# RWKV5 attention and a SoLU feed-forward on one core: the first nine chunks and the first pair written as one flat list of calls, with another order of the first loads

## The chip, the core and the metric

The kernel runs on one core of a Trainium2 chip. A core has a matrix engine (TensorE, PE in the profile, its weight loads PEld), a vector engine (DVE), a scalar engine (ACT), GpSimd (POOL) and a sync engine (SP), which in this kernel only issues DMAs. Each engine runs its own instructions in order and waits on semaphores for the others. The metric is the time of one launch in microseconds on the device.

## The reference

Attention first, then a feed-forward block on its output; B=4 batches, H=8 heads, S=768 steps, D=48 per head, all in float32 but the weights, which the kernel reads as pairs of 32-bit words:

```python
for t in range(S):                       # w: decay per head and dim, u: bonus
    kt, vt, rt = k[:, :, t], v[:, :, t], r[:, :, t]
    cur = einsum('bhd,bhe->bhde', u[None] * kt, vt)
    y[:, :, t] = einsum('bhd,bhde->bhe', rt, state + cur)
    state = w[None, :, :, None] * state + einsum('bhd,bhe->bhde', kt, vt)
x = y.transpose(0, 2, 1, 3).reshape(B * S, H * D)      # 3072 x 384
h = x @ w_in                                           # 3072 x 1024
sm = exp(h - max(h)) / sum(exp(h - max(h)))
solu = h * sm
ln = (solu - mean(solu)) / sqrt(var(solu) + 1e-6) * g_ln
out = ln @ w_out                                       # 3072 x 384
```

## The kernel before

**Tiles.** The 3072 rows are 24 chunks of 128: six stretches of a sequence by four batches, batches inside. Chunk i is worked on by a chain of small functions, each of which puts a few instructions on the engines. The lines are those of the profile.

- `load(i, "kr")` and `load(i, "v")` (L473, L478) put the DMAs of chunk i's k, r and v on SP's queue, into one of five `kpad`, one of five `rpad` and one of six `vt` tiles. k and r are 192 KB each, v is 192 KB, or two halves of 96 KB from chunk 4 on.
- `decay_k(i)` (GpSimd, L702) multiplies k by the table `kdec` into `kp`; `weigh(i)` (GpSimd, L715 and L716) makes `rku` = k·u·r; `sum_own(i)` (DVE, L720) sums it to `own`, the diagonal of the scores. `decay_r(i)` (GpSimd, L709) is used from chunk 9 on.
- `turn_r(i)` and `turn_k(i)` (PE, L759 and L767) transpose r and `kp`; DVE multiplies r by the table `fore` (L760), ACT copies k (L769). From chunk 9 on (`FIRST`), `halve_k`, `halve_r` and `join_rk` do this with a DMA transpose instead.
- `diagonal(i)` writes `own` onto a diagonal in a tile `big`: on ACT, 8 copies at L730, for the first four chunks (`WHOLE`), on GpSimd, 2 selects at L735, for the others.
- `whole_scores(i)` (PE, L782) or `scores(i)` (PE, L800) make the scores in PSUM, in the tile `at`, and `take_scores(i)` (DVE, `copy_predicated`, L808 or L813) copies those above the diagonal into `big`. There is one `at`, with two places used from chunk 8 on: the scores of a later chunk wait until it is read.
- `whole_y(i)` or `merged_y(i)` (PE, L839, L856) make y, ACT copies it (`take_y`, L867). `whole_outer(i)` or `outer(i)` (PE, L892, L883) make the state's increment `kv`; `middle(i)` (DVE, L904) and `update(i)` (DVE, L917, L919, and GpSimd, L922, with the tile `wide`) move the state on.
- `ffn_in(j)` (PE, L932, six matmuls of 128x512) makes h, and ACT its exponential `e` (L937). `unit_a` (DVE, L942, L944) and `unit_b` (ACT, L951, L952) make `solu` and its sums, `deviation` (GpSimd, L960) the deviations.
- `halve_ln(j)` (ACT, L986) splits `solu` in 16-bit halves and sends them through a DMA transpose (L975, on SP's queue), `join_ln(j)` (DVE, L980) puts them together, and `ffn_out(j)` (PE, L1025) multiplies by `w_out` and stores the result.
- The weights come in 14 pieces, 0 to 5 of `w_in` (512 KB each), 6 to 13 of `w_out` (384 KB): `load_weights(p)` (SP, L519), then `convert_a(p)` (ACT, L530, the low words), `convert_b(p)` (DVE, L543 and L545, the high words), `convert_c(p)` (GpSimd, L553, the sum) and, for `w_out`, `convert_d(p)` (the scale of the layer norm, on DVE L564 or ACT L561).
- Before the chunks, DVE builds the tables `back` and `fore` from the decays by repeated squares (L630 to L641), `turn_table` (PE, ACT, L651, L652) turns them to `kdec` and `rdec`, and `spin(n)` (L605) puts n small matmuls with no use of their result on PE.

**Order.** The program says `tc.manual_schedule()`: no planner moves anything. Every engine takes its instructions in the order in which the calls stand in the text, and SP's queue takes the DMAs in that order. The text has these parts: the first loads, the tables, a hand-written list for chunks 0 to 2, a loop over i = 2 to 6 that brings chunks 3 to 7 in and in which the `w_out` pieces are converted, a hand-written list for the first pair (chunks 7 and 8, with chunk 5's and 6's h and the first two results), and a loop over the remaining pairs. The loop over i has, for example,

```python
load(i + 5, "kr")
load(i + 4, "v")
if i > LA:
    ffn_in(j)
```

and so on, so that chunk i+5's loads are issued while chunk i+2's k and r are turned and chunk i-2's h is made. The loads ahead of the first chunks are

```python
load(0, "kr"); load_weights(0); load(1, "kr"); load(0, "v"); load_weights(1); load(2, "kr")
load_weights(2); load(1, "v"); load_weights(3); load_weights(4); load_weights(5)
load(3, "kr"); load(2, "v"); load(4, "kr")
```

(the text has one call to a line). Each is one or two DMAs on SP's queue, and `wq`, the decays, is loaded on the same queue ahead of them.

Of the kernel before, what the change touches and what calls it, by code (L numbers as in the profile page):

```python
# [9 lines left out]
F32 = mybir.dt.float32  # L10
U32 = mybir.dt.uint32
ACT = mybir.ActivationFunctionType
ALU = mybir.AluOpType
# [386 lines left out]
def direct_path(  # L400
# [87 lines left out]
    w_out_sb = const.tile([128, KF, dm], F32, name="w_out_sb")  # L488
    decays = const.tile([128, HP], F32, name="decays")

    nc.vector.memset(wq, 1.0)
    nc.sync.dma_start(out=wq[:, :, 0:D], in_=w.rearrange("(a q) d -> a q d", q=2))
    u_row = u_bc[0:1].rearrange("p h d -> p (h d)")
    nc.scalar.dma_start(out=u_row, in_=u.rearrange("h d -> (h d)").unsqueeze(0))
    for i in range(NLD):
# [20 lines left out]
    def load_weights(j, tag="raw", bufs=6):  # L516
        dst, src, _ = pieces[j]
        raws[j] = wpool.tile([128, dst.shape[1], 2], U32, tag=tag, name="raw", bufs=bufs)
        nc.sync.dma_start(out=raws[j].rearrange("p n o -> p (n o)"), in_=src)  # L519
# [58 lines left out]


    load(0, "kr")  # L580
    load_weights(0)
    load(1, "kr")
    load(0, "v")
    load_weights(1)
    load(2, "kr")
    load_weights(2)
    load(1, "v")
    load_weights(3)
    load_weights(4)
    load_weights(5)  # L590
    load(3, "kr")
    load(2, "v")
    load(4, "kr")
    nc.sync.dma_start(out=g_sb, in_=moe_g_ln.rearrange("(c p) -> p c", p=128))

# [30 lines left out]
    for vt in vts:  # L626
        nc.scalar.activation(out=vt[:, 1].rearrange("p h x -> p (h x)"),
                             in_=ident[:, 0:1].to_broadcast([128, H * P]), func=ACT.Copy, scale=0.0)
    spin(3)
    nc.vector.tensor_scalar(out=pw[:, 0, 0], in0=wd_ps, scalar1=LOW, scalar2=HIGH,  # L630
                            op0=ALU.max, op1=ALU.min)
    nc.vector.tensor_copy(out=decays, in_=wd_ps)
    for j in range(8):
        if j < 7:
            nc.vector.tensor_mul(pw[:, 0, j + 1], pw[:, 0, j], pw[:, 0, j])
# [117 lines left out]
            nc.scalar.copy(out=X["G"][0:D, 1, :, q, :], in_=X["rT"][rows, :, U:T])  # L753

    def turn_r(i):
        rT = factors(i)["rT"]
        ps = psM.tile([128, HP, T], F32, tag="m", name="tr_ps")
        for a in range(HP):
            nc.tensor.transpose(ps[:, a, :], pair(rpads[i % NLD], a), ident)  # L759
        nc.vector.tensor_mul(rT, ps, fore)  # L760

    def turn_k(i):
        X = live[i]
        ps = psM.tile([128, HP, T], F32, tag="m", name="tk_ps")

        for a in range(HP):
            nc.tensor.transpose(ps[:, a, :], pair(X["kp"] if i > 0 else kpads[0], a), ident)  # L767
        if i > 0:
            nc.scalar.copy(out=X["kT"], in_=ps)  # L769
        else:  # L770
            nc.vector.tensor_mul(X["kT"], ps, back)
# [132 lines left out]
            nc.vector.tensor_add(mid(i)[:, :, q], X["kv"][0][q * P : q * P + D],  # L904
                                 carried(i)[:, :, q])

    def update(i):
        b, c = units[i]
        if c == C - 1:
            return  # L910
        X = live[i]
        for q in range(2):
            rows = slice(q * P, q * P + D)
            wT = pw[rows, 0, 7].unsqueeze(2).to_broadcast([D, HP, D])
            new = carried(i + B)[:, :, q]
            if i < WHOLE:
                nc.vector.tensor_mul(new, X["kv"][rows], wT)  # L917
            else:
                nc.vector.tensor_add(new, X["kv"][1][rows], mid(i)[:, :, q])  # L919
        if i >= WHOLE:  # L920
            S = vts[(i + B) % NV][P : P + D, 0, :, 0:D]
            nc.gpsimd.tensor_mul(S, S, wide[P : P + D].unsqueeze(2).to_broadcast([D, H, D]))  # L922


    def ffn_in(i, halves=(0, 1)):
        X = live[i]
        if 0 in halves:
            X["h"] = psH.tile([128, dff], F32, tag="h", name="h_ps")
        h_ps = X["h"]
        for n in halves:  # L930
            for j in range(KD):
                nc.tensor.matmul(h_ps[:, ts(n, NX)], X["xT"][:, j, :], w_in_sb[:, j, ts(n, NX)],  # L932
                                 start=(j == 0), stop=(j == KD - 1))
        if 1 not in halves:
            return
        e = X["e"] = fpool.tile([128, dff], F32, name="e", bufs=1)
        nc.scalar.activation(out=e, in_=h_ps, func=ACT.Exp, accum_out=sums[:, i : i + 1])  # L937

# [41 lines left out]
        nc.vector.tensor_copy(out=words.bitcast(U16).rearrange("p n (t o) -> p o n t", o=2),  # L980
                              in_=turned)

    def halve_ln(i):
        X = live[i]
        both = halves()
        nc.scalar.copy(out=both.rearrange("p (o n) -> p o n", o=2), in_=split(X["solu"]))  # L986
        X["turned"] = turn(both)

    def join_ln(i):
        X = live[i]  # L990
# [49 lines left out]
        for i in chunks:  # L1040
            middle(i)

    ahead = 6

    def take_up(p, more=1):
        nonlocal ahead
        convert_a(p)
        for _ in range(more):
            if ahead < len(pieces):
                load_weights(ahead)  # L1050
                ahead += 1

    turn_r(0)
    turn_k(0)
    turn_table(back, kdec, psM.tile([128, HP, 128], F32, tag="m", name="kd_ps"))
    weigh(0, nc.gpsimd)
    decay_k(0)
    sum_own(0)
    diagonal(0)
    take_up(0)  # L1060
    spin(2)
    whole_scores(0)
    convert_b(0)
    decay_k(1)
    weigh(1, nc.gpsimd)
    turn_r(1)
    spin(4)
    turn_k(1)
    take_scores(0)
    convert_c(0)  # L1070
    sum_own(1)
    take_up(1)
    diagonal(1)
    spin(3)
    whole_y(0)
    whole_outer(0)
    convert_b(1)
    convert_c(1)
    whole_scores(1)
    update(0)  # L1080
    take_y(0)
    decay_k(2)
    weigh(2, nc.gpsimd)
    turn_r(2)
    take_up(2, 0)
    spin(4)
    turn_k(2)
    take_scores(1)
    convert_b(2)
    convert_c(2)  # L1090
    load(5, "kr")
    load(3, "v")
    load(4, "v")
    whole_y(1)
    whole_outer(1)
    whole_scores(2)
    take_up(3)
    take_y(1)
    convert_b(3)
    convert_c(3)  # L1100
    sum_own(2)
    ffn_in(0, (0,))
    take_up(4)
    convert_b(4)
    convert_c(4)
    load(6, "kr")
    load(5, "v")
    take_up(5)
    diagonal(2)
    convert_b(5)  # L1110
    convert_c(5)
    ffn_in(0, (1,))
    update(1)
    take_scores(2)
    decay_k(3)
    whole_y(2)
    whole_outer(2)
    turn_r(3)
    take_y(2)
    turn_k(3)  # L1120
    weigh(3, nc.gpsimd)
    sum_own(3)
    turn_table(fore, rdec, psM.tile([128, HP, 128], F32, tag="m", name="rd_ps"))
    diagonal(3)
    unit(0)
    decay_k(4)
    update(2)
    weigh(4, nc.gpsimd)


    wide = const.tile([128, H], F32, name="wide")
    for q in range(2):
        nc.vector.tensor_copy(out=wide.rearrange("p (a q) -> p a q", q=2)[P : P + D, :, q],
                              in_=pw[q * P : q * P + D, 0, 7])
    todo = list(range(6, len(pieces)))
    now = []
    for i in range(LA, LA + LO):
        j = i - LA
        load(i + 5, "kr")
        load(i + 4, "v")  # L1140
        if i > LA:
            ffn_in(j)
        before, now = now, [todo.pop(0) for _ in range(2 if todo else 0)]
        turn_r(i + 2)
        turn_k(i + 2)
        for p in before:
            convert_c(p)
        for p in now:
            take_up(p)
        if i > LA:  # L1150
            diagonal(i + 1)
            unit(j)
        for p in before:
            convert_d(p, p % 2)
        sum_own(i + 2)
        decay_k(i + 3)
        if i + 3 >= FIRST:
            decay_r(i + 3)
        weigh(i + 3, nc.gpsimd)
        if i - LO >= 0:  # L1160
            halve_ln(i - LO)
        if i - LO - 1 >= 0:
            join_ln(i - LO - 1)
        if i + 1 < WHOLE:
            whole_scores(i + 1)
            take_scores(i + 1)
        else:
            place(i + 1)
            attend([i + 1])
            middle(i + 1)  # L1170
        if LA < i < WHOLE:
            whole_y(i)
            take_y(i)
            whole_outer(i)
        elif i >= WHOLE:
            merged_y(i)
            take_y(i)
        if i > LA:
            update(i)
        else:  # L1180
            nc.vector.tensor_single_scalar(out=minus_g, in_=g_sb, scalar=-1.0, op=ALU.mult)
        if i + 1 >= WHOLE:
            take_scores(i + 1)
        for p in now:
            convert_b(p)
        halve_rk(i + 3)

    checks, checked = list(range(len(pieces))), []

# [10 lines left out]
            decay_r(i)  # L1200
            weigh(i, nc.gpsimd)

    sum_own(FIRST)
    i = LA + LO
    j, l = i - LA, 0
    load(i + 5, "kr")
    decay(i + 3)
    diagonal(i + 1)
    deviation(0, j)
    ffn_in(j)  # L1210
    halve_k(i + 3)
    attend([i + 1], 1)
    unit(j)
    halve_r(i + 3)
    place(i + 1)
    join_ln(l + 1)
    sum_own(i + 3)
    take([i + 1])
    load(i + 4, "v")
    diagonal(i + 2)  # L1220
    decay(i + 4)
    diagonal(i + 3)
    decay(i + 5)
    halve_ln(l + 2)
    join_rk(i + 2)
    ffn_out(l)
    load(i + 6, "kr")
    ffn_in(j + 1)
    unit_a(j + 1)
    load(i + 7, "kr")  # L1230
    update(i)
    update(i + 1)
    join_rk(i + 3)
    ffn_out(l + 1)
    sum_own(i + 4)
    for n in (i, i + 1):
        merged_y(n)
        take_y(n)
    halve_rk(i + 4)
    unit_b(j + 1)  # L1240
    halve_ln(l + 3)
    join_ln(l + 2)
    sum_own(i + 5)

    for i in range(LA + LO + 2, N + LA + LO, 2):
        j, l = i - LA, i - LA - LO
# [113 lines left out]
```

## Time and profile before

| | before |
|---|---|
| time, median of 3 runs | 334.81 us (333.62 to 335.3) |
| profiled execution | 333.98 us, of which the span from first to last instruction is 331.8 |
| granted TensorE clock, mean | 0.994 |
| PE busy | 321.1 us (97%) |
| DVE busy | 222.9 us (67%) |
| ACT busy | 231.1 us (70%) |
| GpSimd busy | 188.4 us (57%) |
| HBM read, written | 26.75 MB, 4.72 MB |
| largest groups on PE | L932 (h) 129.1 us, L1025 (o) 128.3 us |

The profiled execution is one execution; its rows are times in it, counted in us from its first instruction. A line such as "34.91 0.38 SPq L473" gives the start, the duration, the engine and the source line. In the slices, each digit is a fortieth of the span (8.3 us) and the busy share of an engine in it, in tenths.

### The profile page before, as it was taken

How to read it: one execution, taken by the hardware profiler on the slowest of the kernel's cores; microseconds unless marked ns; L12 is line 12 of the kernel's file. 1: busy time of each engine (PE TensorE's matmuls, PEld its weight loads, DVE VectorE, ACT ScalarE, POOL GpSimd, SP SyncE). 2: the span in 40 equal slices, each digit the busy share in tenths (PEclk: the TensorE clock that was granted, in tenths of full speed). 3: DMA queues.
4: the chain of work that ended last, by engine and by line, in shares of the span. 5: the costliest groups of instructions: out<-in, count | busy, mean ns of one | idle time of the engine just before them, and what ended most of it. 6: DMA issues, size and time to landing. Idle time of an engine off the chain costs nothing.

```text
span 331.8 us, 9041 instructions
## 1 busy us (share of the span) xinstructions
PE 321.1 (97%) x3691; PEld 190.1 (57%) x3691; DVE 222.9 (67%) x383; ACT 231.1 (70%) x384; POOL 188.4 (57%) x199
## 2 busy tenths in 40 slices
PE   8989999989999999999999999999999999999992
PEld 5966655545565565565565565565555555555572
DVE  8896999997839867948748848948919415332330
ACT  5776878988489588488488489499496484757420
POOL 6699877799999999697297297292230010100000
PEclk9999999999999999999999999999999999999997
DMA  6999997769999998889978968998558325329941
GB/s 148 241 265 205 202 227 149 130 112 173 187 166 168 183 206 144 166 145 150 204 158 145 221 150 166 178 187 178 122 119 146 93 79 136 65 71 218 200 101 34
DMA packets 165056, 52.59 MB, mean 158 GB/s; under 512 B 158221, under 2 KB 161422, under 8 KB 165006
## 3 DMA queue, kind: packets, MB, share of 16 engines
q1 hardware_dynamic: 165004, 51.92, 79.1%
q8 instruction: 31, 0.51, 0.7%
q14 instruction: 19, 0.16, 0.2%
q10 hardware_dynamic: 2, 0.00, 0.0%
HBM read 26.75 MB, written 4.72 MB: 95 GB/s over the span
## 4 chain that ended last, share of the span: by engine, by line
PE 83%; DVE 6%; ACT 3%; issue 2%; POOL 2%; DMA 2%; POOLq 0%
PE o_ps L1025 38%; PE h_ps L932 32%; PE y_ps L856 5%; PE at L800 3%; PE kv_ps L883 2%; DMA rpad<-in_r_dram 1%; DVE solu L944 1%; POOL kp L702 1%; DVE big L813 1%; DVE ma L545 1%; PE tk_ps L767 1%; POOL rku L716 1%; PE at L782 1%; DMA wq<-in_w_dram 1%; PE y_ps L839 1%
## 5 line engine op out<-in xcount | busy, mean ns | idle before, releaser
L932 PE MATMUL h_ps<-w_in_sb,xT 128*128 128x512 f32 x288 | 129.1, 598 | 0.0
L1025 PE MATMUL o_ps<-w_out_sb,lnT 128*128 128x384 f32 (+1 forms) x400 | 128.3, 476 | 0.0
L1025 PEld LDWEIGHTS o_ps<-w_out_sb,lnT 128*128 128x128 f32 x400 | 74.2, 190 | 48.7 <-issue 4.4
L932 PEld LDWEIGHTS h_ps<-w_in_sb,xT 128*128 128x128 f32 x288 | 53.5, 190 | 61.7 <-issue 57.0
L937 ACT ACTIVATE e<-h_ps 128x1024 f32<-128x1024 f32 x24 | 24.5, 1020 | 35.6 <-PE h_ps L932 35.6
L986 ACT COPY halves<-solu 128x2048 uint16<-128x2048 uint16 x24 | 45.3, 1889 | 1.3 <-DMA halves<-halves 1.3
L922 POOL TENSOR_TENSOR vt<-vt,wide 48x384 f32<-48x384 f32 x16 | 19.6, 1241 | 38.8 <-DVE vt L919 38.4
L980 DVE COPY lnT<-halves 128x2048 uint16<-128x2048 uint16 x24 | 37.2, 1549 | 5.4 <-DMA halves<-halves 5.2
L735 POOL TENSOR_SCALAR_AFFINE_SELECT big<-own 64x512 f32<-64x512 f32 x40 | 36.0, 899 | 2.4 <-PE y_ps L856 0.3
L1027 ACT ACTIVATE o<-o_ps,stats 128x384 f32<-128x384 f32 (+1 forms) x25 | 14.1, 564 | 32.5 <-PE o_ps L1025 20.3
L960 POOL TENSOR_SCALAR stats<-stats 128x2 f32<-128x2 f32 (+2 forms) x11 | 3.8, 343 | 54.7 <-ACT e L952 54.6
L577 DVE TENSOR_REDUCE least<-mag 128x1 f32<-128x384 f32 (+1 forms) x14 | 8.5, 606 | 38.1 <-ACT mag L575 38.1
L702 POOL TENSOR_TENSOR kp<-kpad,kdec 128x512 f32<-128x512 f32 x24 | 31.5, 1315 | 3.8 <-ACT kdec L652 2.4
L944 DVE SCALAR_TENSOR_TENSOR solu<-h_ps,stats,e 128x1024 f32<-128x1024 f32 x24 | 30.8, 1284 | 2.2
L813 DVE COPY_PREDICATED big<-later_half,at 64x512 f32<-64x512 uint32 x40 | 29.6, 739 | 0.7
L951 ACT ACTIVATE solu<-solu,stats 128x1024 f32<-128x1024 f32 x24 | 27.6, 1149 | 2.6 <-DVE solu L944 2.6
L716 POOL TENSOR_TENSOR rku<-rku,rpad 128x384 f32<-128x384 f32 x24 | 27.5, 1148 | 1.9
L942 DVE RECIPROCAL stats<-sums 128x1 f32<-128x1 f32 x24 | 3.9, 161 | 35.4 <-ACT e L937 35.2
L715 POOL TENSOR_TENSOR rku<-kpad,u_bc 128x384 f32<-128x384 f32 x24 | 25.7, 1071 | 1.7 <-ACT u_bc L625 1.7
L952 ACT ACTIVATE e<-solu 128x1024 f32<-128x1024 f32 x24 | 25.4, 1057 | 0.8
L980 DVE COPY big<-halves 128x2048 uint16<-128x2048 uint16 x15 | 22.6, 1508 | 1.9 <-DMA halves<-halves 1.7
L856 PEld LDWEIGHTS y_ps<-big,vt 128*32 128x32 f32 (+1 forms) x1280 | 18.5, 110 | 5.3 <-issue 2.9
(99 smaller groups left out, 384.0 us busy)
## 6 DMA issues: line engine op xcount, KB each, us to landing
raw<-in_moe_w_in_dram SPq DMA_DIRECT2D x12, 512.0 KB, 5.2
raw<-in_moe_w_out_dram SPq DMA_DIRECT2D x16, 384.0 KB, 3.8
kpad<-in_k_dram SPq DMA_DIRECT2D x24, 192.0 KB, 5.3
rpad<-in_r_dram SPq DMA_DIRECT2D x24, 192.0 KB, 5.3
out_dram<-o SPq DMA_DIRECT2D x23, 192.0 KB, 3.7
vt<-in_v_dram SPq DMA_DIRECT2D x40, 96.0 KB, 3.7
vt<-in_v_dram SPq DMA_DIRECT2D x4, 192.0 KB, 6.2
halves<-halves SPq DMA_TRANSPOSE x39, 4.8
```

The source lines that it names most:

```text
L702: nc.gpsimd.tensor_mul(X["kp"].rearrange("p h d -> p (h d)"), kpads[i % NLD].rearrange("p h d -> p (h d)"), kdec.rearrange("p a d -> p (a ...
L715: engine.tensor_mul(rku, kpads[i % NLD][:, :, 0:D], u_bc)
L716: engine.tensor_mul(rku, rku, rpads[i % NLD][:, :, 0:D])
L735: nc.gpsimd.affine_select(out=G[rows, c].rearrange("p a q u -> p (a q) u"), in_=X["own"][rows].to_broadcast([U, H, U]), compare_op=ALU.is_ ...
L813: nc.vector.copy_predicated(X["G"][rows, c].rearrange("p a q u -> p q a u"), later_half[rows].unsqueeze(1).to_broadcast([U, 2, HP, U]), X[ ...
L856: nc.tensor.matmul(y_ps[ts(g, 32), j, ts(c, U)], vf[:, at : at + 32], X["G"][rows, c, h // 2, h % 2, :], start=(g not in opened), stop=las ...
L932: nc.tensor.matmul(h_ps[:, ts(n, NX)], X["xT"][:, j, :], w_in_sb[:, j, ts(n, NX)], start=(j == 0), stop=(j == KD - 1))
L944: nc.vector.scalar_tensor_tensor(out=solu, in0=X["h"], scalar=rs, in1=X["e"], op0=ALU.mult, op1=ALU.mult, accum_out=tot)
L951: nc.scalar.activation(out=solu, in_=solu, func=ACT.Identity, scale=-float(dff), bias=tot)
L980: nc.vector.tensor_copy(out=words.bitcast(U16).rearrange("p n (t o) -> p o n t", o=2), in_=turned)
L986: nc.scalar.copy(out=both.rearrange("p (o n) -> p o n", o=2), in_=split(X["solu"]))
L1025: nc.tensor.matmul(o_ps, X["lnT"][:, f, :], w_out_sb[:, f, part], start=(f == 0), stop=(f == KF - 1))
```

## The change

What the new program does:

- The load of `wq` goes on ACT's DMA queue instead of SP's, ahead of the load of `u`, and the memset of `wq` covers the padding columns alone.
- The first loads are in another order: both k,r pairs and both v's of chunks 0 and 1 early, `w_in` piece 3 ahead of piece 2, chunk 2's v and chunk 3's k and r ahead of pieces 5 and 4.
- `decays` is copied from PSUM first, and the table starts from the copy.
- The list for chunks 0 to 2, the loop over i = 2 to 6 and the list for the first pair are replaced by one flat list of some 300 calls, in which the calls of a function stand at other places relative to the calls of others, and so on each engine. To have more freedom of order, five functions are cut in two: `turn_r` and `grow_r`, `turn_k` and `take_k`, `update` and `fade`, `ffn_in` and `raise_e`, `halve_ln` and `turn_ln`. No instruction is added by the cuts.
- GpSimd's first work on a chunk, `weigh(0)`, stands behind `widen()`, which makes `wide` on GpSimd from the tables `back` and `pw` (it was two copies on DVE after chunk 2). So GpSimd begins when DVE is done with the table.
- On SP's queue, chunk 6's k and r (`load(6, "kr")`) stand behind chunk 7's k and r, one `w_out` piece more, and the v's of chunks 5, 7 and 3; `decay_k(6)` on GpSimd stands ahead of `diagonal(4)`.

The loop over the later pairs is the same. The diff, cut to its core:

```diff
-    nc.vector.memset(wq, 1.0)
-    nc.sync.dma_start(out=wq[:, :, 0:D], in_=w.rearrange("(a q) d -> a q d", q=2))
+    nc.scalar.dma_start(out=wq[:, :, 0:D], in_=w.rearrange("(a q) d -> a q d", q=2))
+    nc.vector.memset(wq[:, :, D:], 1.0)
...
     load(0, "kr")
+    load(1, "kr")
     load_weights(0)
-    load(1, "kr")
     load(0, "v")
+    load(1, "v")
     load_weights(1)
+    load_weights(3)
     load(2, "kr")
+    load(2, "v")
     load_weights(2)
-    load(1, "v")
-    load_weights(3)
+    load(3, "kr")
+    load_weights(5)
     load_weights(4)
-    load_weights(5)
-    load(3, "kr")
-    load(2, "v")
     load(4, "kr")
...
-    nc.vector.tensor_scalar(out=pw[:, 0, 0], in0=wd_ps, scalar1=LOW, scalar2=HIGH,
+    nc.vector.tensor_copy(out=decays, in_=wd_ps)
+    nc.vector.tensor_scalar(out=pw[:, 0, 0], in0=decays, scalar1=LOW, scalar2=HIGH,
                             op0=ALU.max, op1=ALU.min)
-    nc.vector.tensor_copy(out=decays, in_=wd_ps)
...
     def turn_r(i):
-        rT = factors(i)["rT"]
+        factors(i)
...
-        nc.vector.tensor_mul(rT, ps, fore)
+        live[i]["turned_r"] = ps
+
+    def grow_r(i):
+        nc.vector.tensor_mul(live[i]["rT"], live[i]["turned_r"], fore)
...
+        if i >= WHOLE and now:
+            fade(i)
+
+    def fade(i):
         if i >= WHOLE:
             S = vts[(i + B) % NV][P : P + D, 0, :, 0:D]
             nc.gpsimd.tensor_mul(S, S, wide[P : P + D].unsqueeze(2).to_broadcast([D, H, D]))
...
-    wide = const.tile([128, H], F32, name="wide")
-    for q in range(2):
-        nc.vector.tensor_copy(out=wide.rearrange("p (a q) -> p a q", q=2)[P : P + D, :, q],
-                              in_=pw[q * P : q * P + D, 0, 7])
...
+    def widen():
+
+        for q in range(2):
+            rows = slice(q * P, q * P + D)
+            nc.gpsimd.tensor_tensor(out=wide.rearrange("p (a q) -> p a q", q=2)[P : P + D, :, q],
+                                    in0=back[rows, :, 0], in1=pw[rows, 0, 0], op=ALU.mult)
...
+    turn_r(0)
+    turn_k(0)
+    load_weights(8)
+    turn_table(back, kdec, psM.tile([128, HP, 128], F32, tag="m", name="kd_ps"))
+    grow_r(0)
+    take_k(0)
+    whole_scores(0)
+    widen()
+    convert_a(0)
+    weigh(0, nc.gpsimd)
+    sum_own(0)
+    convert_b(0)
+    decay_k(1)
+    diagonal(0)
+    convert_a(1)
+    decay_k(0)
...
+    convert_a(4)
+    convert_b(4)
+    load(7, "kr")
+    load_weights(13)
+    convert_c(4)
+    whole_outer(1)
+    convert_a(5)
+    convert_b(5)
+    load(7, "v")
+    load(3, "v")
+    ffn_in(0, (0,), False)
+    convert_c(5)
+    grow_r(3)
+    diagonal(2)
+    ffn_in(0, (1,), False)
+    take_scores(2)
...
+    turn_table(fore, rdec, psM.tile([128, HP, 128], F32, tag="m", name="rd_ps"))
+    load(6, "kr")
...
+    grow_r(4)
+    scores([4])
+    convert_c(6)
+    take_k(5)
+    grow_r(5)
+    convert_a(8)
+    unit_a(1)
+    convert_d(6, False)
+    decay_k(6)
+    diagonal(4)
+    convert_c(7)
+    place(4)
+    take_scores(4)
+    sum_own(5)
+    outer([4])
+    unit_b(1)
+    middle(4)
...
+    scores([7])
+    join_ln(0)
+    update(6, False)
+    fade(6)
+    merged_y(6)
+    take_y(6)
+    outer([7])
+    middle(7)
+    take_scores(7)
...
```

The cut lines of the list are the other calls for chunks 0 to 12 and for the pieces 2 to 13, then the two `ffn_out` calls of the first pair.

## The prediction

> **What bounds the kernel now.** I read the page's slices first, then busy time by stretch, then the chain, then the DMA issues and the queues around chunk 4. In the slices (40 of 8.3 us each) PE is full from the tenth slice on, DVE from the fifth to the ninth, the DMA engines from the second to the sixth.
>
> ```profile
> PE   8989999989999999999999999999999999999992
> ...
> DVE  8896999997839867948748848948919415332330
> ...
> DMA  6999997769999998889978968998558325329941
> ```
>
> Busy time by stretch (PE, PEld, DVE, ACT, POOL, clock, DMA share, GB/s) says it with numbers: from 30 to 70 us DVE is idle for 0.3 to 0.4 us in ten, PE for up to 0.66, POOL for about 2. The granted clock is 1.00 in each.
>
> ```profile
> 20.00:30.00 10.00, 10.00 (x181) 6.37 (x182) 7.39 (x13) 6.74 (x16) 9.62 (x10) 1.00 0.99 217
> 30.00:40.00 10.00, 9.98 (x132) 6.12 (x130) 9.74 (x21) 8.68 (x20) 8.39 (x8) 1.00 1.12 209
> 40.00:50.00 10.00, 9.77 (x219) 6.44 (x212) 9.70 (x19) 7.81 (x15) 7.71 (x10) 1.00 0.96 213
> 50.00:60.00 10.00, 9.34 (x162) 5.65 (x151) 9.70 (x18) 8.65 (x16) 8.07 (x10) 1.00 0.74 147
> 60.00:70.00 10.00, 9.35 (x151) 5.47 (x150) 9.60 (x18) 8.78 (x15) 8.15 (x10) 1.00 0.89 154
> ```
>
> The chain in order of time gives the hand-over. Until 74.16 it is mostly DVE (and ACT); from 74.20, when the scores of chunk 8 may overwrite what `take_scores(7)` has read, it is PE without a break to the end.
>
> ```profile
> 72.65 0.72 DVE big L813
> ...
> 73.41 0.76 DVE big L813
> 74.16 0.04 issue
> 74.20 0.69 PE at L800 x32
> ...
> 294.54 25.80 PE o_ps L1025 x80
> ```
>
> PE's order behind that point is the same in the new program, and so are its matmuls and its 19 spins. So the change is worth what it does to one moment: when `take_scores(7)` on DVE is done, now 74.16. The profiled execution took 333.98 us (331.8 of span, 2.2 around it); the median of the three runs is 334.81, 0.83 above it. I add the shift to the median.
>
> **The front, to the first h matmul.** Moving `wq` to ACT's queue takes one issue of 0.86 us and its wait off SP: the first k load is issued at 0.8 to 1.1 instead of 1.98, so every load starts about 1.0 earlier (0.9 to 1.2). That GpSimd waits for the table takes `rku` (5.56 to 7.69) out from under the last two table products, which took 2.62 us together; the products before them took 0.19 (128x64) and 0.26 (128x128), a rise that puts the two at 0.40 and 0.68, so the table may be done 0 to 1.5 us sooner. But the PE queue stood there only 0.24 us for it (kd_ps), because transposes and spins were in front. So I walk the queues. ACT: kdec done at 9.9 (10.04 before), then piece 0's convert 0.67, which the list puts ahead of the diagonal, and the diagonal 2.45: 13.0. DVE: `take_scores(0)` 1.37 to 14.4, own 0.55, piece 1 1.38, update 0.72, r of chunk 2 0.69, `take_scores(1)` 1.35: 19.1 against 19.35. PE: y 1.0, r of chunk 3 0.5, scores of chunk 2 1.05, kv 0.35: the first h matmul at 22.0 against 22.27, with chunk 3's r already turned (0.44 of PE). A draw, with some 0.7 in hand. Moving `wide` to GpSimd takes 0.34 off DVE; filling DVE's wait for chunk 3's r (2.43 at 29.76) is worth as much again if nothing else is late. Something is.
>
> **Loads, part one: w_in.** SP's queue lands in order. Before, pieces 3, 4, 5 stood ahead of chunk 3's k and r and chunk 2's v; piece 5 landed at 14.24 + 8.6 = 22.9, and v2 at 18.14 + 8.2 = 26.3. Now those three loads stand ahead of piece 4. The same 17 transfers lie up to v2 before and up to piece 4 now, so piece 4 lands at 26.3 - 1.0 = 25.3, or 24.2 if the thin DMA at 24 to 26 fills up; I take 24.9. Behind it come DVE's two operations for piece 4 (1.4), the same for piece 5 (1.4), and GpSimd's add (1.28): 29.0, where the last add ended at 26.6. The last two h matmuls of chunk 0 (0.43 each) wait for it, and also `diagonal(2)` on ACT, queued behind piece 4's convert. So h of chunk 0 ends near 30.0 against 27.78, and all behind it starts some 2.3 later at 35 us. DVE, which had been 2.4 idle there anyway, absorbs part of this.
>
> **Loads, part two: chunk 6's k.** This is the term that I take to decide. On SP, k7, r7, one w_out piece more, v5 and v7 now go ahead of k6, while on GpSimd `decay_k(6)` has been moved up, ahead of `diagonal(4)`. GpSimd runs in order, so chunk 4's diagonal waits for k6, and DVE's `take_scores(4)` for that diagonal. Before, the k load and GpSimd's two steps stood thus (DMA issue in time and its landing in us; then GpSimd):
>
> ```profile
> 34.91 0.38 SPq L473 DMA_DIRECT2D kpad<-in_k_dram  x1
> ```
> ```profile
> kpad<-in_k_dram SPq DMA_DIRECT2D x1, 192.0 KB, 5.2
> ```
> ```profile
> 40.14 1.38 POOL L735 TENSOR_SCALAR_AFFINE_SELECT big<-own 64x512 f32<-64x512 f32 x2
> 41.60 1.27 POOL L702 TENSOR_TENSOR kp<-kpad,kdec 128x512 f32<-128x512 f32 x1
> ```
> ```profile
> 43.71 1.51 DVE L813 COPY_PREDICATED big<-later_half,at 64x512 f32<-64x512 uint32 x2
> ```
>
> k6 landed at 40.1, the diagonal was made first, and DVE took the scores at 43.71 without a wait. The price of what now stands ahead: the k and r of chunk 7 landed 1.65 us after the load before them (44.5 to 46.1), a v in two halves takes about 1.4 (40.9 to 42.3), so two take 2.8, a w_out piece about 1.3 (37.55 to 38.9). Sum 5.75; with the best spacing of each seen, 4.5; with the worst, 6.5. So k6 lands at 40.1 - 1.0 + 5.75 = 44.8, between 43.4 and 45.7; I take 44.5. kp follows to 45.8, the two selects to 47.1: `take_scores(4)` starts at 47.15, 3.44 late. GpSimd is ready for k6 at 40.0: from the last w_in add at 29.0, three kp (1.28), three rku pairs (2.05) and an add (1.0). So it idles some 4.5 us; the profile gives it 2 us of slack in ten there, and DVE none. Chunk 3's v, one place ahead of k6, lands near 43 and holds y of chunk 3 about 1 us; that lies beside the same wait.
>
> From 43.71 DVE took 30.45 us to the end of `take_scores(7)`. The new order has the same operations behind `take_scores(4)`, and three groups more that DVE had done before it: own 0.53, middle 0.72, update 0.72, together 1.97. So 3.44 + 1.97 = 5.4 late, less what can be got back. In those 30.45 us three L545 took 1.27 instead of 0.56 and two L543 0.79 instead of 0.35, each under a GpSimd operation, and others a little: about 3.2 us. With GpSimd behind, and pieces 10 and 11 set apart, part of it may go: 0 to 3.2, and I take 2.2, the three L545, which are nearest to pairs that the list breaks up. 5.4 - 2.2 = 3.2 us late. PE alone would be there sooner: from h of chunk 1 (32.8, now 35.1) to 74.20 it took 41.4, 1.8 of it idle, so it needs 39.6 and is ready at 74.7. DVE, at 77.4, sets the moment, and nothing behind it gives time back.
>
> A page of the Trainium skill gives another price. "DMA: Bandwidth & Descriptors" (Specifications) puts the fabric's ceiling at 435 GB/s and asks for 512 bytes at least per transfer for line rate; k, r and v move in runs of 192 bytes. At the ceiling 192 KB would be an estimated 0.45 us, the loads put ahead 2.7 instead of 5.75, and the forecast nearly no change (+0.5). The landings of k and r above are 0.8 us apart, and the rows decide.
>
> The rest costs nothing that I can see: splitting `turn`, `take`, `raise_e`, `fade` adds no instruction; the one more dependent copy ahead of the table (decays before pw) is 0.15 us, hidden by what the table gains, and 0.15 on the front if it gains nothing.
>
> **Rivals.** *Faster:* the list fills DVE's 2.43 and loses `wide` (0.34), and k6 comes by 41, since DMA runs fuller in the new order. Then PE's idle time is the bound: 0.23 + 0.66 + 0.65 + 0.29 = 1.8 between 40 and 74, 1.3 at 18 to 19.3: 3.1 in all. I would give 2.0 of it, since DVE is full beside the first part: 332.8. For it: DVE's and PE's gaps are there to take. Against it: DMA at 0.96 to 1.12 busy through 50 us, with more bytes put ahead of k6. It decides if k6 lands before 41. *No change:* k6 lands at 42 to 43, the diagonal at 44.6 to 45.6; then 1.0 to 2.0 late, plus 1.97, less 2.2: about +1.2, 336.0. Or the late start of GpSimd does nothing, because PE's 0.24 us was all there was to get, and the loads do not matter: 0. *Slower by more:* none of the stretch comes back and h of chunk 0 ends at 30: 5.4 and the worst landing, 0.9: up to 341.
>
> **Chances.** A difference under 0.5% (1.7 us) can hardly be told from none here. Slower 0.60 (k6 late: 338.0, own range 336.5 to 341), same 0.19, faster 0.21. The forecast is the likeliest case: 334.81 + 3.2 = 338.0. The range goes from the faster case's middle, 332.8, to 341.0.
>
> **What would show it.** Right: the new profile has GpSimd idle for 3 to 5 us ahead of a kp (line L702), ended by the DMA of kpad, at 39 to 45 us; DVE waits for a select (L735) ahead of its copy_predicated near 47; the last w_in add ends at 29; PE's unbroken stretch begins near 77. Wrong: no such wait on kpad, h of chunk 0 done by 28, and PE's unbroken stretch beginning before 74.2. If kpad waits but the time falls, the DVE sum is the wrong step.

## The result: 3.3% slower

The changed kernel takes 346.75 us (median of 6 runs, 343.46 to 349.79) against 334.98 us (333.62 to 336.31): ratio 1.0329, 95% interval 1.0291 to 1.0367. The ratio leaves out the 349.79 us run, which was in a slower state of the chip, so it lies under the ratio of the two medians. The direction was forecast, the size was not: 11.8 us by the medians instead of 3.2, outside the range. The profiled execution took 348.09 us, of which 346.0 are span; it is 1.3 us above its own median, and the rows below are its rows.

### The profile page after: what moved, and what is told of

It reads as the page before. It is cut to its first block, busy times and chain, and to the rows that moved or that the text cites. A ratio compares the mean times of both kernels' runs of the same rounds, so it can differ in the third digit from the quotient of the medians.

```text
span 346.0 us, 9033 instructions
## 1 busy us (share of the span) xinstructions
PE 325.8 (94%) x3691; PEld 190.5 (55%) x3691; DVE 223.5 (65%) x381; ACT 230.7 (67%) x384; POOL 187.9 (54%) x201
## 4 chain that ended last, share of the span: by engine, by line
PE 64%; DMA 9%; DVE 7%; POOL 7%; SPq 6%; ACT 4%; issue 2%; POOLq 0%; DVEq 0%; ACTq 0%
PE o_ps L1047 29%; PE h_ps L944 27%; PE y_ps L864 4%; DMA halves<-halves 3%; SPq L519 3%; PE at L808 2%; SPq L478 2%; DMA kpad<-in_k_dram 2%; DMA rpad<-in_r_dram 2%; SPq L473 2%; DMA raw<-in_moe_w_in_dram 2%; PE kv_ps L891 2%; POOL kp L702 1%; DVE big L821 1%; POOL big L735 1%
## 5 line engine op out<-in xcount | busy, mean ns | idle before, releaser
L944 PE MATMUL h_ps<-w_in_sb,xT 128*128 128x512 f32 x288 | 132.9, 611 | 4.6 <-ACT xT L875 2.8
L1047 PE MATMUL o_ps<-w_out_sb,lnT 128*128 128x384 f32 (+1 forms) x400 | 128.3, 476 | 0.0
L1047 PEld LDWEIGHTS o_ps<-w_out_sb,lnT 128*128 128x128 f32 x400 | 74.3, 190 | 48.7 <-issue 3.5
L944 PEld LDWEIGHTS h_ps<-w_in_sb,xT 128*128 128x128 f32 x288 | 54.6, 194 | 69.0 <-issue 58.4
L1002 ACT COPY halves<-solu 128x2048 uint16<-128x2048 uint16 x24 | 45.4, 1891 | 4.7 <-DMA halves<-halves 4.6
L934 POOL TENSOR_TENSOR vt<-vt,wide 48x384 f32<-48x384 f32 x16 | 18.3, 1159 | 41.0 <-DVE vt L927 40.8
L821 DVE COPY_PREDICATED big<-later_half,at 64x512 f32<-64x512 uint32 x40 | 29.5, 739 | 6.1 <-POOL big L735 5.6
L716 POOL TENSOR_TENSOR rku<-rku,rpad 128x384 f32<-128x384 f32 x24 | 28.2, 1175 | 1.9
L715 POOL TENSOR_TENSOR rku<-kpad,u_bc 128x384 f32<-128x384 f32 x24 | 26.4, 1098 | 0.1
```

What stands on the lines that cost most here:

```text
L715: engine.tensor_mul(rku, kpads[i % NLD][:, :, 0:D], u_bc)
L716: engine.tensor_mul(rku, rku, rpads[i % NLD][:, :, 0:D])
L821: nc.vector.copy_predicated(X["G"][rows, c].rearrange("p a q u -> p q a u"), later_half[rows].unsqueeze(1).to_broadcast([U, 2, HP, U]), X[ ...
L1047: nc.tensor.matmul(o_ps, X["lnT"][:, f, :], w_out_sb[:, f, part], start=(f == 0), stop=(f == KF - 1))
```

## The profile after

The slices first (40 of 8.65 us): PE, DVE, the clock and DMA. PE, full from the tenth slice on before, has a hole in the fifteenth, and two before that (sixth, seventh); DVE has one in the sixth and in the tenth; the clock is below full in the seventh and the sixteenth, behind PE's holes, where before it was full all through the stretch.

```profile
PE   5998977999999979999999999999999999999983
...
DVE  6777949996968936992982883975937606332330
...
PEclk9999998999999998999999999999999999999999
DMA  9999999833987999896996896987576436329931
```

In the new file the functions have other lines: L808 is `scores`, L821 `take_scores`, L847 `whole_y`, L875 `take_y`, L944 h, L1002 `halve_ln`, L991 its DMA transpose, L1047 the result. Chunk 6's k with its r is called k6 from here on, chunk 3's v v3.

From the waits up to 100 us (who waited for whom; us in total, times, longest):

```profile
...
POOL kp L702 <- DMA kpad<-in_k_dram: 5.7, 1, 5.7
DVE big L821 <- POOL big L735: 5.6, 2, 5.1
...
ACT low L530 <- DMA raw<-in_moe_w_out_dram: 4.9, 1, 4.9
...
PE y_ps L847 <- DMA vt<-in_v_dram: 2.6, 1, 2.6
```

The first two are the wait that was forecast: GpSimd stands for chunk 6's k, and DVE for the select behind it. The other two stand in the same stretch: ACT for w_out piece 11, PE for chunk 3's v. The chain shows how late k6 is; then come the kp and the first select:

```profile
41.17 6.39 DMA kpad<-in_k_dram
...
47.70 1.26 POOL kp L702
48.96 0.62 POOL big L735
```

DVE's `take_scores(7)` ends at 81.90 (74.16 before) and chunk 8's scores start at 82.39 (74.20): 8.2 us. Before, these scores waited for DVE:

```profile
74.20 0.69 PE L800 MATMUL at<-big 48*64 48x64 f32 x32 [0.29 <-DVE big L813]
```

After, they did not; they follow on an h of PE's own, and DVE was done 0.5 us earlier:

```profile
77.05 5.42 PE L944 MATMUL h_ps<-w_in_sb,xT 128*128 128x512 f32 x12
82.39 0.69 PE L808 MATMUL at<-big 48*64 48x64 f32 x32
```

PE's last wait ahead of them is one of 0.82 us for DVE, and it ends at 57.96; the h behind it takes 7.11 us instead of 5.42. The other 6.3 us are lost behind that point, where the same rows took 251.65 us before and take 258.0 now. The chain at 121 us says where:

```profile
121.17 4.64 DMA halves<-halves
...
125.86 1.78 issue
127.64 0.57 ACT o L1049
128.21 0.38 ACT xT L875
...
128.64 7.11 PE h_ps L944 x12
```

ACT waits 4.6 us for a DMA transpose whose buffer it needs, PE waits 2.51 us for ACT's copies behind that, and then twelve matmuls that take 5.4 us elsewhere take 7.11. The busy time by stretch shows why (PE, PEld, DVE, ACT, POOL, then the granted clock, DMA share and GB/s):

```profile
125.00:130.00 5.00, 2.49 (x84) 1.64 (x74) 0.00 (x0) 4.17 (x5) 2.86 (x4) 0.99 1.19 141
130.00:135.00 5.00, 5.00 (x9) 2.11 (x8) 4.48 (x5) 3.82 (x8) 2.47 (x3) 0.67 0.99 215
```

PE's pause is followed by a clock of 0.67. The rest of the 6.3 us is mostly 1.72 us ahead of the last check, where the last transpose took 6.96 us; an execution of b_newfirst below, which is the program before with other first loads, has such a wait too (1.83 us), and those of a_k6, a_diag and a_k14, which are the changed program there, have none. So it is not put down to the change.

## The experiments

Each kernel is compared with the kernel before on the same chip; "above" is the ratio of the runs less one, with its 95% interval. "At 8" is the start of chunk 8's scores in the one profiled execution, "rest" the time from there to the last matmul.

| kernel | median us | above | at 8 | rest |
|---|---|---|---|---|
| before | 334 to 335.3 | | 74.20 | 251.65 |
| after | 346.75 | 3.29% (2.91 to 3.67) | 82.39 | 258.00 |
| a_k6 | 347.21 | 3.81% (3.37 to 4.26) | 83.21 | 258.18 |
| a_diag | 346.43 | 3.90% (3.72 to 4.07) | 78.62 | 256.42 |
| a_k14 | 342.87 | 2.63% (2.40 to 2.86) | 83.96 | 251.64 |
| a_three | 342.50 | 2.52% (2.26 to 2.78) | 83.94 | 252.26 |
| a_oldsp | 347.41 | 3.83% (3.19 to 4.46) | 82.11 | 256.88 |
| a_oldlater | 343.72 | 2.44% (2.08 to 2.80) | 81.37 | 255.67 |
| b_newsp | 338.70 | 1.13% (0.76 to 1.51) | 78.75 | 251.65 |
| b_newfirst | 336.70 | 0.60% (0.39 to 0.81) | 77.25 | 255.29 |
| a_wq | 342.40 | 2.53% (2.17 to 2.89) | 81.75 | 252.08 |
| a_v3 | 339.23 | 1.51% (1.16 to 1.86) | 79.19 | 252.16 |
| a_v3wq | 341.06 | 1.93% (1.64 to 2.21) | 80.82 | 252.05 |
| b_late | 334.78 | -0.14% (-0.37 to 0.08) | 74.02 | 252.02 |
| a_w45 | 338.73 | 1.25% (1.06 to 1.44) | 79.41 | 252.09 |
| a_w45x | 336.50 | 0.73% (0.47 to 1.00) | 77.68 | 252.37 |
| a_w45wq | 338.04 | 0.99% (0.76 to 1.22) | 77.93 | 253.20 |
| b_k14 | 335.77 | 0.43% (0.18 to 0.68) | 74.55 | 252.82 |
| a_v3only | 340.82 | 2.15% (1.78 to 2.51) | 80.99 | 252.33 |
| a_v3c11 | 337.34 | 0.93% (0.65 to 1.21) | 79.01 | 252.19 |

"At 8" and "rest" are of one execution each, and executions of one kernel differ by some us in all (343.46 to 348.09 of the changed one; a_diag's row is of its fastest run, b_newfirst's of its slowest); the verdicts rest on the ratios.

### a_k6, a_diag, a_k14, a_three: is it chunk 6's k, and what is the loss at 121?

```diff
 # a_k6                        # a_diag              # a_k14
+    load(6, "kr")             +    diagonal(4)      +    load(14, "kr")
     load(7, "kr")                  decay_k(6)            ffn_out(0)
...                            -    diagonal(4)      ...
-    load(6, "kr")                                   -    load(14, "kr")
```

> The changed program with the load of chunk 6's k and r put ahead of chunk 7's k and r on SP's queue, nothing else. Theory (GpSimd's wait for k6 holds chunk 4's diagonal and so DVE): 1152 KB less stand ahead of k6, so it lands near 42 instead of 47.6, the 5.7 us wait ahead of GpSimd's kp falls under 1 us, DVE's wait of 5.1 us ahead of the fourth take_scores goes, and chunk 8's scores start near 77.5 instead of 82.4: 341.5 to 342.5 us against 346.75. Rival (the w_out pieces and v's, which are late as well, set the same stretch): the wait moves to a raw piece or a v and less than 1.5 us is gained: 345 or more.

> The changed program with chunk 4's diagonal put back ahead of chunk 6's kp on GpSimd; the loads stay as they are. Theory: the selects are made at 42.0 to 43.4, DVE takes chunk 4's scores at about 44.5 instead of 49.6, and GpSimd still waits for k6 until 47.6 but with only kp of chunk 6 behind it, which PE turns at 53: 342 to 343 us. Rival (k6 is late for everything, so its order against the diagonal does not matter; GpSimd's adds for the w_out pieces behind it hold DVE and ACT): 345 or more.

> The changed program with the load of chunk 14's k and r put ahead of the first result's matmuls (it stood at the end of the first pair, behind the second and third DMA transposes of the feed-forward). Theory (SP's queue, with k14 and r14 pressed in front of the next pair's loads, delays the DMA transposes; ACT waits 4.6 us for one of them at 121 and PE 2.5 us for ACT, after which the clock falls to 0.67 for 5 us, 1.7 us): both go, 342 to 343.5 us. Rival (the wait at 121 comes from the late start of the whole, not from k14's place): within 1 us of 346.75.

> All three of the edits before together. Theory (two separate losses, of about 8.2 us up to chunk 8's scores, some 5 of it by k6, and 4.2 at 121 to 135): 337 to 338.5 us, still above the kernel before by what the front lost. Rival (the losses overlap, one hides the other): no better than the better of the single ones, 341 or more.

As the one cause, k6's wait fell at once: with k6 early, or with the select ahead of kp, the waits on `kpad` and on the select are gone (at most 0.5 us is left), and the time is not lower. Only chunk 14's place gave something, 0.66% or 2.2 us, with "rest" back at 251.64. What takes k6's place is seen in PE's timeline of a_three (start, us; in brackets the idle time before and what ended it):

```profile
48.82 1.94 PE L847 MATMUL y_ps<-big,vt 128*32 128x128 f32 x32 [5.18 <-DMA vt<-in_v_dram]
...
51.33 6.54 PE L944 MATMUL h_ps<-w_in_sb,xT 128*128 128x512 f32 x12
```

Chunk 3's v stands behind k6 on SP's queue, and what is put ahead of it makes it later: PE waits 5.18 us instead of 2.57, and again the twelve matmuls behind the pause are long. In a_k6 it waits 4.09 us there.

Chunk 14's place is read in SP's queue. After:

```profile
111.81 0.54 SPq L473 DMA_DIRECT2D kpad<-in_k_dram  x1
112.41 0.56 SPq L473 DMA_DIRECT2D rpad<-in_r_dram  x1
...
117.89 3.17 SPq L478 DMA_DIRECT2D vt<-in_v_dram  x4
121.17 6.61 SPq L991 DMA_TRANSPOSE halves<-halves  x2
```

and a_k14:

```profile
98.76 0.53 SPq L473 DMA_DIRECT2D kpad<-in_k_dram  x1
99.34 0.57 SPq L473 DMA_DIRECT2D rpad<-in_r_dram  x1
...
115.33 3.17 SPq L478 DMA_DIRECT2D vt<-in_v_dram  x4
118.61 8.45 SPq L991 DMA_TRANSPOSE halves<-halves  x3
```

With k14 and r14 at the end of the pair's list, the next pair's transposes are issued 38.8 us after chunk 8's scores begin; with them ahead of the first result, 34.7, where the kernel before has 34.3.

### a_oldsp, b_newsp, b_newfirst, a_oldlater: the order of the loads, or of the engines?

The loads from the first to chunk 14's are put in the old order on the new engines' list, or the other way round; each call keeps its place and takes the next load of the other order.

```diff
 # b_newsp: at every place of a later load in the program before
-        load(i + 5, "kr")
-        load(i + 4, "v")
+        following()     # the next of: raw 8, 9, 7, k5, raw 6, v4, v5, k7, raw 13, v7, v3, k6, ...
+        following()
```

> The changed program's order on every engine, with the old order of loads on SP's queue from the first to chunk 14's (the calls stand at the same places of the list, each takes the next load of the old order; wq on SP's queue again). The single edits of k6 and of chunk 4's diagonal gained nothing, since chunk 3's v and the w_out pieces then came late. Theory (the order of loads as a whole costs what was lost, the engines' order is a draw): 333 to 337 us. Rival (the engines' order loses by itself: GpSimd begins late, and the list does not fit any order of loads): 341 us or more.

> The other corner: the program before on every engine, with the changed order of loads on SP's queue from the first to chunk 14's, and wq on ACT's queue. Theory (the order of loads costs it): 342 to 350 us. Rival (the engines' order costs it): 334 to 337 us.

> The program before with only the first loads changed: wq on ACT's queue and the new order up to chunk 4's k and r. Theory (the front's part of the loss, piece 4 behind v2, k3 and r3, is about 3 us at the first h and is half absorbed by DVE's idle time behind it): 335 to 337 us. Rival (an earlier start of the loads pays for it): 333 to 334.5 us.

> The changed program with the old order of the later loads (from the first w_out piece to chunk 14), the new first loads kept. Theory (nearly all of the loss is in the later loads): 335 to 338.5 us. Rival (the first loads and the late front hold most of it): 342 us or more.

Neither the loads nor the engines' order is the whole of it; b_newfirst came out as its theory said. The new order of loads costs the old engines 1.13%, of which the first loads are 0.60%; the old later loads win the new list 0.85% of its 3.29%. So the order of loads loses in both lists, and how much depends on the list it stands in; what the engines' order loses by itself these runs do not settle. Chunk 14's load is the last in both orders, so its place among the calls is not exchanged: it stays late in a_oldlater and a_oldsp, and early in b_newsp. a_oldsp tells nothing apart: in the new list PE turns chunk 3's r ahead of chunk 0's h, and with the old first loads it stood 5.55 us for r3 at 26.

### a_wq, a_v3, a_v3wq, b_late: the parts by themselves

All but b_late have chunk 14's load put forward as in a_k14; a_v3 has k6 and the diagonal put back too.

```diff
 # a_v3, beside the three edits above
+    load(3, "v")
     load(4, "v")
...
     load(7, "v")
-    load(3, "v")
 # a_wq
-    nc.scalar.dma_start(out=wq[:, :, 0:D], ...)
+    nc.sync.dma_start(out=wq[:, :, 0:D], ...)
 # b_late, the program before
+    wide, made on GpSimd from back and pw
     weigh(0, nc.gpsimd)
```

> The changed program with chunk 14's load put forward as in a_k14 and wq loaded on SP's queue again, so that u is the first DMA on ACT's queue. In the changed program wd_ps starts at 4.34 instead of 3.23, u's matmul at 5.53 instead of 3.34 and kdec at 10.97 instead of 9.45. Theory (wq on ACT's queue makes wq 1.1 and u 2.2 us later, and the front with it): the first scores start 1 us sooner, and 0.5 to 1.5 us of the time go against 342.87: 341.4 to 342.4. Rival (every load starts 1 us later for it, and the stretch behind is bound by the loads): 342.9 to 344.

> The changed program with chunk 14's load put forward, chunk 3's v ahead of chunk 4's, chunk 6's k and r ahead of chunk 7's, and chunk 4's diagonal ahead of chunk 6's kp. With the last two alone, y of chunk 3 waited 4 to 5 us for chunk 3's v. Theory (k6 and v3 hold the same stretch, one behind the other, so that only both together give something): y of chunk 3 does not wait, chunk 8's scores start near 78.5 instead of 82 to 84, 338.5 to 340 us. Rival (the w_out pieces, then later still, take their place): 341.5 us or more.

> a_v3 and a_wq together. Theory (the front and the loads of k6 and v3 add up): 337.5 to 339 us. Rival (either hides the other): as the better of the two.

> The program before with one part of the change alone: GpSimd makes wide from the tables ahead of its first weigh, so it begins when DVE is done with the table, and DVE's two copies for wide go. Theory (the last two products of the table take 0.39 and 0.70 us instead of 1.22 and 1.37, GpSimd's rku ends 2 us later but the first diagonal is made at most 0.5 us later): within 0.8 us of the kernel before. Rival (rku is late for own and the first diagonal, and the whole front is late by it): 336 to 337.5 us.

a_v3 bears out that v3 and k6 hold the same stretch: together they give 1.1% (2.63 to 1.51, the intervals are apart), k6 and the diagonal without v3 0.1%. wq's queue makes no difference that can be told (2.53% against 2.63%), and with a_v3 it is no gain either. GpSimd's late start is a draw in the program before.

### a_w45, a_w45x, a_w45wq, b_k14: what is left

```diff
 # a_w45: old first loads, and in the list          # a_w45x, besides
-    turn_r(3)                                      -    convert_a(11)
     whole_scores(2)                                     whole_y(3)
...                                                      take_y(3)
     update(1, False)                               ...
+    turn_r(3)                                           raise_e(2)
+    grow_r(3)                                      +    convert_a(11)
```

> a_v3 with the old order of the first loads (w_in pieces 3, 4, 5 ahead of chunk 3's k, r and chunk 2's v; wq stays on ACT's queue), and chunk 3's turn_r and grow_r moved behind chunk 2's y, since r3 now comes later. In a_v3 the last w_in add ends at 30.4 and h of chunk 0 at 31.6; before it was 27.8, and chunk 8's scores start 5.0 us later than before. Theory (the late pieces 4 and 5 are what is left): h of chunk 0 ends near 28.5, chunk 8's scores start at 76 to 77, 335.5 to 337 us. Rival (DVE is the bound behind it and takes the 3 us back as idle time): 338.5 us or more.

> a_w45 with ACT's convert of w_out piece 11 moved behind chunk 2's exponential; it stands ahead of chunk 3's copy of y and waited 3.8 us for its load in a_v3, and PE 1.5 us for that copy. Theory: 0.5 to 1.5 us less than a_w45. Rival (PE waits for DVE's scores there anyway): the same.

> a_w45x with wq on SP's queue again. Theory (wq and u come 1 to 2 us sooner, the front with them): 0.5 to 1 us less than a_w45x, and the engines' order is then a draw with the kernel before: 334 to 336 us. Rival (the loads, which start 1 us later, cost as much): the same or 1 us more.

> The program before with one edit: chunk 14's k and r are loaded behind the last DMA transpose of the first pair instead of behind its first result's h. Theory (SP's queue then brings the next pair's transposes late, whatever stands on the engines): 337 to 339.5 us. Rival (the old order has the slack to hide it): within 0.8 us of the kernel before.

In a_w45 h of chunk 0 ends at 29.22 (31.60 in a_v3), and next to nothing of it reaches the end (1.25% against 1.51%), because ACT stands:

```profile
52.13 0.55 ACT L530 ACTIVATE low<-raw 128x384 uint32<-128x384 uint32 x1 [5.99 <-DMA raw<-in_moe_w_out_dram]
52.59 0.46 ACT L875 COPY xT<-y_ps 128x384 f32<-128x384 f32 x1
```

The copy of chunk 3's y waits behind a convert whose piece has not landed. Moved away (a_w45x), 0.5% more is gone, and the intervals are apart. wq on SP's queue again does not help (0.99%, overlapping). b_k14 shows chunk 14's place in the program before: 0.43%, 1.4 us, between what theory and rival said; ACT waits 3.9 us for the transpose there, PE 1.1.

### a_v3only, a_v3c11: two sizes

> The changed program with chunk 14's load put forward and chunk 3's v ahead of chunk 4's; chunk 6's k and the order of chunk 4's diagonal and chunk 6's kp stay as changed. Theory (v3 and k6 hold the same stretch, each enough by itself): GpSimd still waits for k6 for some 6 us and DVE for the select, 341.5 to 343 us, near a_k14's 342.87. Rival (v3 alone was the loss and k6's wait costs nothing of its own): 338.5 to 340 us, as a_v3.

> a_v3 with ACT's convert of piece 11 moved behind chunk 2's exponential, the new first loads kept. It differs from a_w45x only by the first loads and the place of chunk 3's turn_r. Theory (late pieces 4 and 5 start h of chunk 1 some 2.6 us later, and DVE, idle in parts of the stretch, takes back about half): 337.5 to 338.5 us, 1 to 2 above a_w45x. Rival (their delay is hidden in full): 336.5 us.

With v3 alone put forward, the wait that the prediction named is still there:

```profile
POOL kp L702 <- DMA kpad<-in_k_dram: 4.3, 1, 4.3
...
DVE big L821 <- POOL big L735: 3.8, 1, 3.8
```

and the time is 2.15% above the kernel before; without it 1.51% (a_v3). So k6's wait seems to have a part of its own, some 2 us, but the intervals overlap a little. a_v3c11, with the new first loads, is 0.93% above against 0.73% for a_w45x: the first loads cost less than its theory said, and the difference is within the noise. In a row, in us of 335: chunk 14's place 2.2, v3 1.6, k6 with the diagonal 2.1, piece 11's convert 1.9, the first loads 0.7. That is 8.6 of 11.0. Clear of the noise are chunk 14's place (narrowly) and v3 with k6 taken together, and the convert between a_w45 and a_w45x; the other single steps have intervals that overlap. 2.4 us are left in a_w45x. They are not settled: PE still stands 2.5 us there for ACT's copy of chunk 6's k, ahead of which the moved convert now waits, and the h behind it takes 7.1 us. No version beat the kernel before.

## Why the prediction was wrong

**The wait was right; what came last was another engine, by 0.5 us.** GpSimd stood 5.72 us ahead of kp, ended by the DMA of `kpad`, forecast 3 to 5; the last w_in add ended at 29.81, forecast 29.0; piece 4, forecast to land at 24.9, let DVE begin at 25.65; h of chunk 0 ended at 30.99, forecast 30.0. PE's stretch was to begin near 77, with the end of DVE's `take_scores(7)`, and PE alone was to be ready at 74.7. It began at 82.4, and PE came last, behind DVE's 81.90, with an h of 7.11 us on the way. DVE's lateness had reached PE earlier, in its waits up to 57.96.

**k6's landing: 44.5 forecast, 47.56 measured.** Two terms were off. The lead of 1.0 us from the earlier start had shrunk to 0.4 when `g`, the last of the first loads, landed (28.7 against 29.1). And from there to k6's landing it took 18.8 us instead of 11.0, so what was put ahead, priced at 5.75 from the spacings of the old queue, took 7.8. The DMA engines moved less in the new order, as two stretches show against 208 and 254 GB/s before:

```profile
25.00:30.00 5.00, 3.99 (x10) 1.38 (x9) 4.24 (x7) 3.59 (x10) 3.15 (x4) 1.00 0.83 158
35.00:40.00 5.00, 5.00 (x43) 2.65 (x43) 4.96 (x8) 4.97 (x13) 4.51 (x5) 1.00 0.78 150
```

Why was not tried by itself. SP's queue stood 4.24 us in the issue of `g`, from 21.54 (0.90 us before); but the old order has an issue as long, 4.35 us for chunk 2's v at 18.14, and its first w_out piece was issued later, at 26.34 against 25.91. `take_scores(4)` started at 49.60, 5.89 late, not 3.44.

**The stretch given back: 2.2 forecast, 0.1 measured.** From `take_scores(4)` to the end of `take_scores(7)` DVE took 32.30 us; 30.45 and the 1.97 of the three groups moved behind it make 32.42. The slow products of the weights were not freed: they lay under other GpSimd instructions (L543 took up to 1.21 us, 0.79 before). 5.89 + 1.97 - 0.12 is the 7.74 that DVE was late.

**One wait was taken for the cause where several ended within a few us of each other.** The sum walked one chain and put the others, v3's 1 us among them, "beside the same wait". That is true of a wait that ends first, and it means too that the first edit that removes one can gain nothing: putting k6 right gave nothing that can be told (a_k6, a_three); v3 gave 1.6 us, and behind it k6 2.1 and piece 11 1.9. Piece 11's convert alone was not tried. For the sum that is no error, since the longest wait counts; for the size of the loss it is one, because the queue that brought k6 late brought the others late too: v3, forecast near 43, let y of chunk 3 start at 45.86.

**"Nothing behind it" was wrong.** The matmuls behind chunk 8's scores are the same, but not what stands on SP's queue between them. Chunk 14's load was moved from ahead of the second result to the end of the list, past two transposes. The prediction did not walk that queue; it cost 2.2 us by the ratios, and in the profiled execution 2.5 us of pause and 1.7 of slow matmuls. That term was left out of the range too, but it is not the whole of what the range missed: without it (a_k14) the time is still 342.87, above 341.0.

**The clock was not priced.** The prediction noted 1.00 and added none. The mean clock of the six runs after is 0.986 to 0.995, of the kernel before, in the set of runs that varied most, 0.991 to 1.000. One h at 0.82 to 0.84 took 7.11 instead of 5.42, another at 0.67 took 7.11: 1.7 us each in the profiled execution.

**The front.** First h at 24.02, not 22.0. The table went as worked out: its last two products took 0.39 and 0.70 without GpSimd, forecast 0.40 and 0.68. What was missed is that `wq` on ACT's queue comes 1.1 us later and pushes `u`, which follows it, by 2.2:

```profile
4.34 0.23 PE L622 MATMUL wd_ps<-ident,wq 4*128 4x4 f32 x1 [1.28 <-DMA wq<-in_w_dram]
5.53 1.61 PE L624 MATMUL u_ps<-u_bc,ones_row 1*128 1x384 f32 x2 [0.96 <-DMA u_bc<-in_u_dram]
```

They stood at 3.23 and 3.34. In a_wq, with `wq` back on SP's queue, the time is the same within the noise, so none of this is seen at the end.

The price by the Trainium skill's page "DMA: Bandwidth & Descriptors" (Specifications), nearly no change, was further off than the rows, and on the same side: its estimate for the loads put ahead was 2.7 us, the rows gave 5.75, and they took 7.8.

## What to carry to other kernels

In this kernel one queue brings nearly everything, and an order that made one load late made several engines wait at once. In such a case removing the wait that the profile names first may gain nothing until the next two are gone too, so read all the waits that end in the same few microseconds, and undo them together before one by one. Walk the load queue to the end of the region that a change touches, DMA transposes included, even where the bounding engine's own order is unchanged. And price a pause of the matrix engine with the slow matmuls that may follow it, here up to 1.7 us.

## What the runs showed of the hardware

A pause of PE can cost more than its length. In the profiled execution after, PE paused 2.51 us; its first matmuls then came 0.43 us apart, as elsewhere, and the next four 0.85. The granted clock was 0.50 from 130.3 to 133.0, and 0.78 and 0.84 in the 0.9 us before and the 1.0 us behind. The page "TensorE: Matmul & The Clock Gate" of the Trainium skill (Part 1) says that the clock goes to half after an idle window of some 3.4 us and back after a busy one, and that the window runs freely, so that it differs between executions. The half rate agrees with the 0.85 us, and so does the length of the slow stretch: the rows add up to some 3.4 us at half rate (0.9 us at a mean of 0.78 is 0.4 us of it), and they do so again at 58 us (0.66 from 57.9 to 58.9, 0.50 to 61.0, 0.68 to 62.0). Half of that, 1.7 us, is what each of the two h lost. The length of the pause does not quite agree: pauses of 0.99 and 0.82 us close together stood ahead of the slow matmuls at 58 us, while one of 2.57 us at 43 had none behind it. And a longer pause cost no more: behind one of 4.65 us in a_k6 the h took 6.96 us.
